# Small products in TensorE's first gaps, a later place for w_out's decode and the spatial tail's split, and another buffer for u's last weight chunk

## The chip, the cores and the metric

The kernel runs on one core of a Trainium2 chip. The metric is the device time in microseconds (us), taken as the median of several executions. Engines are named as in the profile: PE (TensorE matmul), PEld (its weight loads), DVE (VectorE), ACT (ScalarE), POOL (GpSimd) and SP (SyncE, which issues all the DMAs here).

## The reference

```python
def _attn_ref(q, k, v, g_norm):             # (8, 8, 576, 64)
    kv = np.einsum('bhsd,bhse->bhde', k, v)
    out = np.einsum('bhsd,bhde->bhse', q, kv)
    rms = np.sqrt(np.mean(out * out, axis=-1, keepdims=True) + 1e-06)
    return out / rms * g_norm

def _moe_ref(x, w_in, w_spatial, b_spatial, w_out):   # x: (8, 576, 512)
    h = np.maximum(x @ w_in, 0.0)
    u, v = h[..., :d_ff // 2], h[..., d_ff // 2:]
    v_n = (v - mean(v)) / np.sqrt(var(v) + 1e-06)
    v_s = np.einsum('ts,bsd->btd', w_spatial, v_n) + b_spatial[None, :, None]
    return (u * v_s) @ w_out
```

Linear attention without a softmax, eight batches of eight heads, normalized by head; then a gated network on the eight heads side by side: a product with `w_in` (512 x 1024), a layer norm of its second half v, a product with the 576 x 576 spatial weights along the sequence, the gate u times that, and a product with `w_out` (512 x 512). `w_in` and `w_out` are 64-bit floats and are handed over as raw words.

## The kernel before

**Stages.** One batch after the other. For a batch b and a pair of heads p: `att_k` multiplies k by v (`pskv`, L128) and copies the result to SBUF (L131, L132); `att_qa` multiplies q by it (`pso`, L188), squares it (ACT L171 by head with an accumulated sum, or L174 with a DVE sum L175) and begins the inverse root (L150 to L152); `att_qb` finishes it and scales (L157 to L159, x at L180); `att_t` transposes x on PE (`pstr`, L216) and copies it to SBUF (L218 for batch 0, L209 and L210 later). The last 64 rows of a pair of batches go together (`pst`, `pstt`). Then `hv` makes v and its layer norm, `u_unit` makes u, `sp_steps` the spatial product, `out_unit` the product with `w_out`.

**Batch 0** is computed another way, in plain fp32, while the weights still come in: `hv_32` (`psh`, L355) takes one 128-row chunk k of x and of `w_in` and adds it to four banks, one for each 128 tokens c; `u_32` (`psu`, L379) does the same for u; `sp_32` (`psa`, L388, L389) uses the spatial weights as they were loaded. From batch 1 on each product is three products of high and low halves (L272, L305, L411), and the halves are made by a copy on ACT and a subtraction on DVE: `split_in` (L566, L567) for `w_in`, `split_ws` for the spatial weights, `split_tail` (L605 to L614) for the spatial weights' last 64 rows and the bias, `make_out` for `w_out`.

**Weights.** `weight64` decodes a chunk of 64-bit words to fp32: one ACT instruction (L557) and five on DVE (L558 to L562), for each of eight chunks of `w_in` (four for v, then four for u) and four of `w_out`. A chunk is loaded into a staging buffer: `stage1` (four buffers) takes v's chunks and then the spatial weights, `stage0` (two) u's chunks, `stage2` (one) u's third chunk and then each of the four chunks of `w_out`. When batch 0 is done, `gates` closes `stage0` and `stage1` and puts the gate's halves (`GH`, `GL`) and `w_out`'s (`WOH`, `WOL`) in their place.

**What sets the order.** `PLAN`, a string of tokens, calls these steps for batch 0 in the order written: J, K are `att_k`; A, D `att_qa` (D with the squares summed on ACT); B `att_qb`; T `att_t`; H `hv_32` (H30 is tokens 3, chunk 0); u `u_32`; s `sp_32`; W the next weight load; C the next decode; X, E, z the splits; P `gates`; R the split of u's gate; L allows one more load of q, k or v; N8 is eight products of a zero tile before anything has come in. A scheduler then orders each engine's instructions by its own model: an instruction that depends on little can stand much earlier than its place in the program. An instruction given to `tc.keep_in_program_order` stays behind those so marked before it on its engine. On the chip each engine runs its list in order, and SP issues the DMAs in its own order.

Of the kernel before, what the change touches and what calls it, by code (L numbers as in the profile page):

```python
# [8 lines left out]
F32 = mybir.dt.float32  # L9
F32R = mybir.dt.float32r  # L10
U32 = mybir.dt.uint32
I32 = mybir.dt.int32
AF = mybir.ActivationFunctionType
ALU = mybir.AluOpType
# [3 lines left out]
DM, FF = 512, 1024  # L18
FH = FF // 2
P = 128  # L20
NP = H // 2
NC = S // P
TAIL = S - NC * P
# [8 lines left out]
HALF = DM // 2  # L32
NB = B
PLAN = """
N8 W L J00 D00 L W G J01 B00 C A01 L W L J02 T00 H00 C H10 H20 H30 B01 W C D02 J03 T01 Z H01 H11 H21 H31 C
L W B02 D03 T02 H02 H12 H22 H32 W B03 C d0 T03 H03 H13 H23 H33 b0 W L e0 e1 e2 e3 C L K10 C W t0 K11 C
u00 u01 u02 u03 F0 L K12 F1 W W L K13 F2 W W W d1 b1 F3 u10 X0 u11 X1 u12 L A10 X2 u13 t1 X3 L B10 A11 h E0
T10 s L B11 E1 T11 s A12 s L B12 z X4 s T12 A13 X5 s B13 L X6 s T13 W L X7 s s P R
"""


def f32(ap):
    return ap.bitcast(F32)
# [3 lines left out]
def body(ctx: ExitStack, tc, qT, kvm, kvt, g2, w_in, wsT, bsp, w_out, out):  # L47
    nc = tc.nc
    w_in = w_in.bitcast(U32)
    w_out = w_out.bitcast(U32)  # L50
# [9 lines left out]
    def persistent(shape, dt, name):  # L60
        return const.tile(shape, dt, name=name, tag=name)
# [10 lines left out]
    WTH = persistent([P, S], F32R, "WTH")  # L72
    WTL = [persistent([P, S], F32R, f"WTL{i}") for i in range(2)]
# [4 lines left out]
    R = [vpool.tile([P, 14 * HF], F32, name=f"R{x}", tag=f"V{x}") for x in "HL"]  # L78
# [7 lines left out]
    KVB = [persistent([P, P], F32, f"KVB{i}") for i in range(2)]  # L86
# [208 lines left out]
    def hv(b, c):  # L295
        ps = ps_mm.tile([P, 512], F32, name="psh", tag="mm")
        for k in range(NP):
            hv_k(c, k, ps)
        hv_end(c, ps)
# [7 lines left out]
    def split(hi, lo, x):  # L307
        nc.scalar.copy(hi, x)  # L308
        nc.vector.tensor_tensor(lo, x, f32(hi), op=ALU.subtract)  # L309
# [26 lines left out]
    def hv_tail():  # L336
        ps = ps_mm.tile([P, 512], F32, name="psh", tag="mm")
        cols = slice(NT, XC)
        three(ps, [m for k in range(NP) for m in
                   hl(XH[:, k, cols], XL[:, k, cols], WIH[:, k, FH:FF], WIL[:, k, FH:FF])])  # L340
        v = work.tile([P, FH], F32, name="v", tag="v", bufs=3)
        layer_norm(ps, v, nc.vector)
        d = work.tile([P, HS], F32, name="d", tag="g")[:, 0:HF]
        nc.vector.tensor_tensor(d, v[:, 0:HF], v[:, HF:FH], op=ALU.subtract)
        for x, cols in (v, slice(0, FH)), (d, slice(FH, FH + HF)):
            for i in range(2):
                own = slice(i * TAIL, (i + 1) * TAIL)
                other = slice((1 - i) * TAIL, (2 - i) * TAIL)
                hi = TA[i][own, cols]
                nc.scalar.copy(hi, x[own])  # L350
                nc.vector.tensor_copy(TB[i][own, cols], x[own])
                nc.vector.tensor_tensor(TA[i][other, cols], x[own], f32(hi), op=ALU.subtract)
# [31 lines left out]
    def sp_32(d, j):  # L384
        ps = ps_mm.tile([P, 512], F32, name="psa", tag="mm")[:, 0:HS]
        ds, cols = slice(d * P, (d + 1) * P), slice(j * HS, (j + 1) * HS)
        for c in range(NC):
            nc.tensor.matmul(ps, V32[:, c, ds], staged["s", c][:, cols], start=c == 0, stop=False)  # L388
        nc.tensor.matmul(ps, VT32[0:TAIL + 1, ds], WT32[0:TAIL + 1, cols], start=False, stop=True)  # L389
        nc.vector.tensor_tensor(U[:, d, cols], ps, U[:, d, cols], op=ALU.mult)  # L390
# [130 lines left out]
    GH = GL = WOH = WOL = None  # L521
    stage2 = ctx.enter_context(tc.tile_pool(name="stage2", bufs=1))
    staging = [ExitStack(), ExitStack()]
    stage0 = staging[0].enter_context(tc.tile_pool(name="stage0", bufs=2))
    stage1 = staging[1].enter_context(tc.tile_pool(name="stage1", bufs=4, side="right"))
    V32 = stage0.tile([P, NC, FH], F32, name="V32", tag="V32", bufs=1)
    WT32 = stage0.tile([P, S], F32, name="WT32", tag="WT32", bufs=1)
    staged, psu = {}, {}

    def load64(src, i, pool):  # L530
        staged[i] = pool.tile([P, 2 * DM], U32, name="stage", tag="stage")
        nc.sync.dma_start(staged[i], src)

    def load_in(half, k):
        i = NP * (1 - half) + k
        load64(w_in[k * P:(k + 1) * P, 2 * half * FH:2 * (half + 1) * FH], i,
               stage1 if half else stage2 if k == 2 else stage0)

    def load_ws(c):
        staged["s", c] = stage1.tile([P, 2 * DM], F32, name="stage", tag="stage")  # L540
        nc.sync.dma_start(staged["s", c][:, 0:S], wsT[c * P:(c + 1) * P, :])

    def load_tail():
# [2 lines left out]
            nc.sync.dma_start(WT32[r:r + 1], bsp)  # L546

    def load_out(k):
        load64(w_out[k * P:(k + 1) * P, :], 2 * NP + k, stage2)

    def weight64(i):

        wide = staged.pop(i).rearrange("p (f two) -> p f two", two=2)
        w0, w1 = wide[:, :, 0], wide[:, :, 1]
        to = W32[i] if i < 2 * NP else f32(w1)
        t = work.tile([P, DM], U32, name="t", tag="stg", bufs=2)
        nc.scalar.activation(f32(t), f32(w1), AF.Abs, scale=2.0 ** -112)  # L557
        nc.vector.tensor_scalar(t, t, 3, None, op0=ALU.logical_shift_left)  # L558
        nc.vector.scalar_tensor_tensor(w1, w1, 0x80000000, t, op0=ALU.bitwise_and, op1=ALU.bitwise_or)
        nc.vector.tensor_scalar(t, w1, 0xFF800000, None, op0=ALU.bitwise_and)  # L560
        nc.vector.scalar_tensor_tensor(f32(w0), w0, 2.0 ** -52, f32(t), op0=ALU.mult, op1=ALU.mult)
        nc.vector.tensor_tensor(to, f32(w1), f32(w0), op=ALU.add)  # L562
        return to

    def split_w(hi, lo, x):
        tc.keep_in_program_order(nc.scalar.copy(hi, x))  # L566
        tc.keep_in_program_order(nc.vector.tensor_tensor(lo, x, f32(hi), op=ALU.subtract))  # L567
# [3 lines left out]
        split_w(WIH[:, n % NP, fs], WIL[:, n % NP, fs], W32[n])  # L571

    def make_out(k):
        split_w(WOH[:, k, :], WOL[:, k, :], weight64(2 * NP + k))

    def split_ws(k):

# [24 lines left out]

    def split_tail():
        rows, other, r = slice(0, TAIL), slice(TAIL, P), TAIL + 32
        tc.keep_in_program_order(nc.scalar.copy(WTH[rows], WT32[rows]))  # L605
        nc.vector.tensor_tensor(WTL[0][rows], WT32[rows], f32(WTH[rows]), op=ALU.subtract)
        nc.scalar.copy(WTH[other], WT32[rows])
        nc.scalar.copy(WTL[1][other], f32(WTL[0][rows]))
        for n in (TAIL, r):
            nc.scalar.copy(WTL[0][n:n + 1], WT32[n:n + 1])  # L610
        low = WTL[0][r:r + 1]
        nc.vector.tensor_tensor(low, WT32[r:r + 1], f32(low), op=ALU.subtract)
        for n in (TAIL, r):
            nc.scalar.copy(WTL[1][n - TAIL:n - TAIL + 1], f32(WTL[0][n:n + 1]))  # L614

    todo = [(b + (kind != "f"), p, kind) for b in range(0, B, 2) for kind in "fkq"
            for p in range(NP)]
# [9 lines left out]
    def ahead(n=1):  # L627
        wanted[0] += n
        issue()
# [11 lines left out]
    def warm(n):  # L641

        ps = ps_tail.tile([P, 512], F32, name="psw", tag="tail")
        for _ in range(n):
            nc.tensor.matmul(ps[:, 0:P], KVB[1], KVB[1], start=True, stop=True)

    queue = []

    def enqueue(b, late=0):
# [3 lines left out]
    def step(n=1):  # L653
        for _ in range(n):
            if queue:
                queue.pop(0)()

    def gates():
        nonlocal GH, GL, WOH, WOL
        staging[0].close()  # L660
        pool = ctx.enter_context(tc.tile_pool(name="gates", bufs=1))
        GH, GL = (pool.tile([P, 4, XC], F32R, name=n, tag=n) for n in ("GH", "GL"))
        staging[1].close()
        outw = ctx.enter_context(tc.tile_pool(name="outw", bufs=1, side="right"))
        WOH, WOL = (outw.tile([P, NP, DM], F32R, name=n, tag=n) for n in ("WOH", "WOL"))

    loads = [lambda k=k: load_in(1, k) for k in range(NP)]
    loads += [lambda k=k: load_in(0, k) for k in range(NP)]
# [5 lines left out]
    psv = [ps_mm.tile([P, 512], F32, name="psh", tag="mm") for _ in range(NC)]  # L674
    st = [states.setdefault(b, {}) for b in range(2)]
    do = {
        "N": warm,
        "L": lambda: ahead(), "W": lambda: loads.pop(0)(), "C": lambda: weight64(makes.pop(0)),
        "K": lambda b, p: att_k(b, p, st[b]), "A": lambda b, p: att_qa(b, p, st[b]),
        "B": lambda b, p: att_qb(b, p, st[b]), "T": lambda b, p: att_t(b, p, st[b]),  # L680
# [5 lines left out]
        "F": lambda c: normalize(V32[:, c], nc.vector),  # L686
        "G": lambda: nc.sync.dma_start(gcol, g2), "h": hv_tail_32, "u": u_32,
        "s": lambda: sp_32(*units.pop(0)), "X": split_in, "E": split_ws, "z": split_tail,
        "Z": blank_tails, "P": gates, "R": split_g,
    }  # L690
    for token in PLAN.split():
        do[token[0]](*map(int, token[1:]))
# [3 lines left out]
    def first(b):  # L696

        for c in (0, 2, 1, 3):
            hv(b, c)
            step()  # L700
        for d in range(4):
            if d == 1 and b % 2 == 0:
                step(len(queue))
                hv_tail()
            elif d == 2 and b % 2:
                enqueue(b + 1)
                enqueue(b + 2)
            for j in range(2):
                u_unit(b, d, j)
                step()  # L710
            if b == 1:
                make_out(d)
                if loads:
                    loads.pop(0)()
    def second(b):
# [5 lines left out]
    def last(b):  # L721
        for c in [0, 1] + [NC] * (b % 2) + [2, 3]:
            out_unit(b, c)
            step()

    first(1)
    last(0)
    second(1)
# [53 lines left out]
```

## Time and profile before

| | us |
|---|---|
| median of 3 runs | 531.82 |
| the runs | 531.82, 529.98, 1777.45 |
| the profiled execution | 531.08 |
| its span, first to last instruction | 529.3 |
| mean granted clock of TensorE in it | 0.984 |

In a timeline row stand the start and the busy time (us), the engine, the source line, the operation, output <- input, the shape and the count; in brackets, how long the engine was idle before and what released it. A row of stages has the stretch and its length, the busy time (and instructions) of PE alone or of PE, PEld, DVE, ACT and POOL, the granted clock of TensorE, the busy share of the DMA engines and GB/s.

### The profile page before, as it was taken

Reading aid. Unit: us, or ns where it says so; the run is one execution under the profiler, and the core shown is the slowest. Engines: PE = TensorE matmul, PEld = TensorE weight load, DVE = VectorE, ACT = ScalarE, POOL = GpSimd, SP = SyncE. Lnnn points to the kernel's source line nnn. Section 1 sums busy time; section 2 is a strip of 40 time slices with the busy share of each in tenths; the row PEclk is TensorE's granted clock in tenths of the full one; section 3 lists DMA queues with packets and bytes.
Section 4 is the critical chain, followed back from the end, with each engine's and each line's share of the span. In section 5 each row is a group of like instructions: output and inputs, shape, how many; then the busy total and the mean of one; then the engine's idle time right before and its main releaser. Section 6 shows DMA issues by size and latency. Waiting matters only on the chain.

```text
span 529.3 us, 9377 instructions
## 1 busy us (share of the span) xinstructions
PE 514.7 (97%) x3496; PEld 449.6 (85%) x3496; DVE 359.9 (68%) x1089; ACT 241.5 (46%) x629; POOL 9.1 (2%) x25
## 2 busy tenths in 40 slices
PE   6978999999999999999999999999999999999997
PEld 5635867798998899989998899979998889988995
DVE  2799299879692697828693489918586289937480
ACT  3494365555542364335443356424444256334321
POOL 5000000000000000000000000000000000000000
PEclk8689999999999999999999999999999999999999
DMA  8963310242407102020424401120432300010003
GB/s 265 358 204 133 106 40 23 63 162 99 159 12 253 41 1 63 24 79 23 163 81 149 152 20 26 42 79 1 157 108 70 132 20 15 8 63 18 0 2 100
DMA packets 22305, 46.50 MB, mean 88 GB/s; under 512 B 2866, under 2 KB 7474, under 8 KB 22260
## 3 DMA queue, kind: packets, MB, share of 16 engines
q1 hardware_dynamic: 22260, 45.91, 26.4%
q8 instruction: 27, 0.44, 0.3%
q14 instruction: 18, 0.15, 0.1%
HBM read 36.46 MB, written 9.44 MB: 87 GB/s over the span
## 4 chain that ended last, share of the span: by engine, by line
PE 87%; DVE 7%; DMA 2%; ACT 2%; issue 1%; SPq 0%; ACTq 0%; DVEq 0%
PE pso L272 19%; PE psu L272 17%; PE psh L305 13%; PE psb L411 5%; PE pso L188 5%; PE psa L411 4%; PE pskv L128 4%; PE psc L411 4%; PE psu L379 2%; PE pstr L216 2%; PE psa L388 2%; PE psh L355 2%; PE psh L272 2%; DMA stage<-w_out 1%; PE pst L141 1%; DMA KV<-kvm 1%
## 5 line engine op out<-in xcount | busy, mean ns | idle before, releaser
L272 PE MATMUL psu<-XH,WIH 128*128 128x288 f32 x224 | 66.9, 299 | 0.0
L272 PE MATMUL psu<-XL,WIH 128*128 128x288 f32 x224 | 66.1, 295 | 0.0
L272 PE MATMUL psu<-XH,WIL 128*128 128x288 f32 x224 | 66.0, 295 | 0.0
L272 PE MATMUL pso<-WOH,GH 128*128 128x512 f32 x144 | 58.3, 406 | 0.2
L272 PE MATMUL pso<-WOL,GH 128*128 128x512 f32 x144 | 56.6, 394 | 0.0
L272 PE MATMUL pso<-WOH,GL 128*128 128x512 f32 x144 | 54.3, 396 | 0.0
L284 DVE BATCH_NORM_STATS2 s<-v 128x6 f32<-128x512 f32 x32 | 22.0, 692 | 41.8 <-ACT v L278 41.6
L438 ACT CAST GH<-g 128x288 fp32r<-128x288 f32 (+2 forms) x84 | 26.3, 351 | 42.7 <-DVE g L430 42.6
L305 PE MATMUL psh<-WIH,XH 128*128 128x512 f32 x112 | 44.4, 397 | 0.0
L305 PE MATMUL psh<-WIL,XH 128*128 128x512 f32 x112 | 43.8, 391 | 0.0
L305 PE MATMUL psh<-WIH,XL 128*128 128x512 f32 x112 | 42.8, 391 | 0.0
L272 PEld LDWEIGHTS psu<-XH,WIH 128*128 128x128 f32 x224 | 42.0, 188 | 0.7
L272 PEld LDWEIGHTS psu<-XL,WIH 128*128 128x128 f32 x224 | 42.0, 188 | 0.2
L272 PEld LDWEIGHTS psu<-XH,WIL 128*128 128x128 f32 x224 | 42.0, 188 | 0.0
L402 ACT ACTIVATE U<-psu 128x288 f32<-128x288 f32 x56 | 23.0, 411 | 33.4 <-PE psu L272 32.5
L512 ACT COPY o<-pso 128x512 f32<-128x512 f32 x35 | 19.7, 588 | 40.0 <-PE pso L272 37.7
L309 DVE TENSOR_TENSOR VL<-v,VH 128x512 fp32r<-128x512 f32 (+1 forms) x56 | 33.7, 617 | 6.2 <-ACT VH L308 5.7
L175 DVE TENSOR_REDUCE ss<-x 128x8 f32<-128x512 f32 x35 | 23.8, 681 | 19.1 <-ACT x L174 18.8
L308 ACT CAST VH<-v 128x512 fp32r<-128x512 f32 (+1 forms) x56 | 30.4, 564 | 11.1 <-DVE v L331 5.5
L272 PEld LDWEIGHTS pso<-WOH,GL 128*128 128x128 f32 x144 | 27.0, 188 | 5.7
L272 PEld LDWEIGHTS pso<-WOH,GH 128*128 128x128 f32 x144 | 27.0, 188 | 5.4 <-DVE g L430 0.6
L272 PEld LDWEIGHTS pso<-WOL,GH 128*128 128x128 f32 x144 | 27.1, 188 | 4.6
(185 smaller groups left out, 1228.5 us busy)
## 6 DMA issues: line engine op xcount, KB each, us to landing
KV<-kvm SPq DMA_DIRECT2D x31, 512.0 KB, 4.5
out<-o SPq DMA_DIRECT2D x32, 256.0 KB, 2.1
qt<-qT SPq DMA_DIRECT2D x16, 288.0 KB, 2.9
stage<-w_in SPq DMA_DIRECT2D x8, 512.0 KB, 6.9
qt<-qT SPq DMA_DIRECT2D x16, 256.0 KB, 2.6
KT<-kvt SPq DMA_DIRECT2D x32, 64.0 KB, 4.8
stage<-w_out SPq DMA_DIRECT2D x4, 512.0 KB, 3.4
stage<-wsT SPq DMA_DIRECT2D x4, 288.0 KB, 6.2
```

Of the source, the lines that this page charges most:

```text
L128: nc.tensor.matmul(ps[h, h], of[:, 0, h], of[:, 1, h], start=c == 0, stop=c == NC)
L175: nc.vector.tensor_reduce(ss, heads(x), axis=AX.X, op=ALU.add)
L188: nc.tensor.matmul(ps[:, c * P:(c + 1) * P], qt[:, c * P:(c + 1) * P], st[p], start=True, stop=True)
L272: nc.tensor.matmul(ps, lt, rh, start=i == 0, stop=i == n - 1)
L284: nc.vector.bn_stats(s6, v)
L305: nc.tensor.matmul(ps, lt, rh, start=k == 0 and i == 0, stop=k == NP - 1 and i == 2)
L308: nc.scalar.copy(hi, x)
L309: nc.vector.tensor_tensor(lo, x, f32(hi), op=ALU.subtract)
L402: nc.scalar.activation(U[:, d, cols], ps[:, 0:HS], AF.Relu)
L411: nc.tensor.matmul(ps, lt, rh, start=start and i == 0, stop=stop and i == len(pairs) - 1, skip_group_check=True)
L438: nc.scalar.copy(GH[:, d, dst], g[:, src])
L512: nc.scalar.copy(o, ps)
```

## The change

1. A new step `filler(n)`, token n: n products of 128 x 128 of the tile `KVB[1]` with itself, into the first 128 columns of the bank that `hv_32` uses for tokens 3 and has not begun. `PLAN` has n6 behind J00, n8 behind D00, n6 behind J01 and n6 behind A01. `KVB[1]` is zero until J01 has copied its product into it.
2. `PLAN` moves D02 and D03 to other places, moves weight loads (W), and puts the w_out chunks 0 and 1 in it: Q0 and Q1 (`make_out`, now the decode alone) before X0 and behind X5, O0 and O1 (`split_out`) behind P. The decodes of chunks 2 and 3 stay in `first(1)`.
3. The first two instructions of the decode of w_out's chunks 0 and 1, and all of `split_tail`, are marked to stay in program order; two of its copies change places.
4. Buffers: u's fourth chunk goes to `stage1` and not `stage0`; the fourth spatial chunk and w_out's chunk 1 go to `stage0`. `gates` is cut in two: `outw` (P) closes `stage1` and makes `WOH`, `WOL`; `gates` (p), behind the splits O0 and O1, closes `stage0` and makes `GH`, `GL`.

```diff
-N8 W L J00 D00 L W G J01 B00 C A01 L W L J02 T00 H00 C H10 H20 H30 B01 W C D02 J03 T01 Z H01 H11 H21 H31 C
+N8 W L J00 n6 D00 L n8 W G J01 n6 B00 C A01 L n6 W L J02 T00 H00 H10 D02 C H20 H30 B01 W C J03 T01 Z H01 H11 D03 H21 H31 W C
...
-               stage1 if half else stage2 if k == 2 else stage0)
+               stage2 if i == NP + 2 else stage1 if half or k == 3 else stage0)
...
+        pool = stage1 if c < 3 else stage0
...
-        load64(w_out[k * P:(k + 1) * P, :], 2 * NP + k, stage2)
+        load64(w_out[k * P:(k + 1) * P, :], 2 * NP + k, stage0 if k == 1 else stage2)
...
-        nc.scalar.activation(f32(t), f32(w1), AF.Abs, scale=2.0 ** -112)
-        nc.vector.tensor_scalar(t, t, 3, None, op0=ALU.logical_shift_left)
+        keep = tc.keep_in_program_order if i in (2 * NP, 2 * NP + 1) else lambda ins: ins
+        keep(nc.scalar.activation(f32(t), f32(w1), AF.Abs, scale=2.0 ** -112))
+        keep(nc.vector.tensor_scalar(t, t, 3, None, op0=ALU.logical_shift_left))
...
-        split_w(WOH[:, k, :], WOL[:, k, :], weight64(2 * NP + k))
+        decoded[k] = weight64(2 * NP + k)
+
+    def split_out(k):
+        split(WOH[:, k, :], WOL[:, k, :], decoded.pop(k))
...
+    def filler(n):
+        for _ in range(n):
+            tc.keep_in_program_order(
+                nc.tensor.matmul(psv[3][:, 0:P], KVB[1], KVB[1], start=True, stop=True))
...
+    def outw():
+        nonlocal WOH, WOL
         staging[1].close()
...
-            if b == 1:
-                make_out(d)
+            if b == 1 and d < 2:
+                make_out(2 + d)
+                split_out(2 + d)
```

PE at the program's start, from the first product of k and v (J00) to the second product of q (A01); `KVB_95` and `KVB_96` are `KVB[0]` and `KVB[1]`. Rows with a + are new:

```order
 L128 MATMUL pskv<-KT_103 64x64 x2
+L656 MATMUL psh<-KVB_96 128x128 x6
 L188 MATMUL pso<-KVB_95,qt 128x128 x4
 L141 MATMUL pst<-KVB_95,qt 128x128
+L656 MATMUL psh<-KVB_96 128x128 x8
 L128 MATMUL pskv<-KV_102 64x64 x8
 L128 MATMUL pskv<-KT_104 64x64 x2
+L656 MATMUL psh<-KVB_96 128x128 x6
 L188 MATMUL pso<-KVB_96,qt 128x128 x4
 L141 MATMUL pst<-KVB_96,qt 128x128
+L656 MATMUL psh<-KVB_96 128x128 x6
```

Four blocks, 26 products, now stand between the attention products; the third reads `KVB[1]` behind J01 and so takes J01's copied product, not zeros.

ACT before, from the decode of a u chunk to the copy of the last transposed chunk of batch 0 (RH is x of batch 0, WT the loaded spatial tail):

```order
L557 ACTIVATE t<-stage 128x512
L607 CAST WTH<-WT_121 64x576
L610 CAST WTL_81<-WT_121 1x576 x2
L218 ACTIVATE RH<-pstr,gcol 128x512
L171 ACTIVATE x,ss<-pst 128x64 x8
L614 CAST WTL_82<-WTL_81 1x576 x2
L566 CAST WIH<-RL 128x512
L150 ACTIVATE sh<-ss,epsc 128x8
L557 ACTIVATE t<-stage 128x512 x2
L218 ACTIVATE RH<-pstr,gcol 128x512
```

The same place of the changed kernel, from the decodes of u's last two chunks on:

```order
L559 ACTIVATE t<-stage 128x512 x2
L171 ACTIVATE x,ss<-pso 128x64 x8
L218 ACTIVATE RH<-pstr,gcol 128x512
L171 ACTIVATE x,ss<-pst 128x64 x6
L150 ACTIVATE sh<-ss,epsc 128x8
L171 ACTIVATE x,ss<-pst 128x64 x2
L150 ACTIVATE sh<-ss,epsc 128x8
L218 ACTIVATE RH<-pstr,gcol 128x512
```

The tail's casts (L607 to L614), one split of `w_in` (L566) and the second of the two decodes (L557 x2, the first chunk of w_out) are gone from between the two copies of RH; the squares of D03 now stand ahead of the first of them.

SP before, from the third load of k and v (for J02) to the fourth (for J03) and the load of `w_in` behind it:

```order
L108 DMA KV_101<-kvm 128x1024
L109 DMA KT_103<-kvt 64x256
L118 DMA qt<-qT 128x576
L532 DMA stage<-w_in 128x1024
L108 DMA KV_102<-kvm 128x1024
L109 DMA KT_104<-kvt 64x256
L532 DMA stage<-w_in 128x1024
```

and in the changed kernel:

```order
L108 DMA KV_101<-kvm 128x1024
L109 DMA KT_103<-kvt 64x256
L532 DMA stage<-w_in 128x1024 x2
L118 DMA qt<-qT 128x576
L532 DMA stage<-w_in 128x1024 x2
L113 DMA qs<-qT 128x128
L532 DMA stage<-w_in 128x1024
L108 DMA KV_102<-kvm 128x1024
L109 DMA KT_104<-kvt 64x256
L532 DMA stage<-w_in 128x1024
```

Five loads of `w_in`, of half a megabyte each, now stand between the two loads of k and v, where one stood. From the second batch's spatial product on, the engines' lists are the same in both kernels.

More of the change, by code (lines that the diff above doesn't have):

```diff
@@ L34 @@
 PLAN = """
-N8 W L J00 D00 L W G J01 B00 C A01 L W L J02 T00 H00 C H10 H20 H30 B01 W C D02 J03 T01 Z H01 H11 H21 H31 C
-L W B02 D03 T02 H02 H12 H22 H32 W B03 C d0 T03 H03 H13 H23 H33 b0 W L e0 e1 e2 e3 C L K10 C W t0 K11 C
-u00 u01 u02 u03 F0 L K12 F1 W W L K13 F2 W W W d1 b1 F3 u10 X0 u11 X1 u12 L A10 X2 u13 t1 X3 L B10 A11 h E0
-T10 s L B11 E1 T11 s A12 s L B12 z X4 s T12 A13 X5 s B13 L X6 s T13 W L X7 s s P R
+N8 W L J00 n6 D00 L n8 W G J01 n6 B00 C A01 L n6 W L J02 T00 H00 H10 D02 C H20 H30 B01 W C J03 T01 Z H01 H11 D03 H21 H31 W C
+W B02 L T02 H02 H12 H22 H32 W B03 C W d0 T03 H03 H13 H23 H33 b0 e0 e1 e2 e3 C L K10 C t0 L K11 C
+u00 u01 u02 u03 F0 L K12 F1 W W L K13 F2 W W W W d1 b1 F3 u10 Q0 u11 X0 u12 L A10 X1 u13 t1 X2 L B10 A11 h X3
+T10 s L B11 E0 T11 s A12 s L B12 E1 z s T12 A13 X4 W s B13 L X5 Q1 s T13 X6 L s X7 s P O0 O1 p R W
 """
@@ L527, in body @@
     WT32 = stage0.tile([P, S], F32, name="WT32", tag="WT32", bufs=1)
-    staged, psu = {}, {}
+    staged, decoded, psu = {}, {}, {}
     def load64(src, i, pool):
@@ L536, in load_in @@
         load64(w_in[k * P:(k + 1) * P, 2 * half * FH:2 * (half + 1) * FH], i,
-               stage1 if half else stage2 if k == 2 else stage0)
+               stage2 if i == NP + 2 else stage1 if half or k == 3 else stage0)
     def load_ws(c):
-        staged["s", c] = stage1.tile([P, 2 * DM], F32, name="stage", tag="stage")
+        pool = stage1 if c < 3 else stage0
+        staged["s", c] = pool.tile([P, 2 * DM], F32, name="stage", tag="stage")
         nc.sync.dma_start(staged["s", c][:, 0:S], wsT[c * P:(c + 1) * P, :])
@@ L604, in split_tail @@
         rows, other, r = slice(0, TAIL), slice(TAIL, P), TAIL + 32
[L605 to L608, printed above, removed]
+        keep = tc.keep_in_program_order
+        low = WTL[0][r:r + 1]
+        keep(nc.scalar.copy(WTH[rows], WT32[rows]))
+        keep(nc.vector.tensor_tensor(WTL[0][rows], WT32[rows], f32(WTH[rows]), op=ALU.subtract))
+        keep(nc.scalar.copy(WTH[other], WT32[rows]))
         for n in (TAIL, r):
-            nc.scalar.copy(WTL[0][n:n + 1], WT32[n:n + 1])
-        low = WTL[0][r:r + 1]
-        nc.vector.tensor_tensor(low, WT32[r:r + 1], f32(low), op=ALU.subtract)
+            keep(nc.scalar.copy(WTL[0][n:n + 1], WT32[n:n + 1]))
+        keep(nc.vector.tensor_tensor(low, WT32[r:r + 1], f32(low), op=ALU.subtract))
+        keep(nc.scalar.copy(WTL[1][other], f32(WTL[0][rows])))
         for n in (TAIL, r):
-            nc.scalar.copy(WTL[1][n - TAIL:n - TAIL + 1], f32(WTL[0][n:n + 1]))
+            keep(nc.scalar.copy(WTL[1][n - TAIL:n - TAIL + 1], f32(WTL[0][n:n + 1])))
     todo = [(b + (kind != "f"), p, kind) for b in range(0, B, 2) for kind in "fkq"
@@ L658, in gates @@
     def gates():
-        nonlocal GH, GL, WOH, WOL
+        nonlocal GH, GL
         staging[0].close()
@@ L662, in gates @@
         GH, GL = (pool.tile([P, 4, XC], F32R, name=n, tag=n) for n in ("GH", "GL"))
+    def outw():
+        nonlocal WOH, WOL
         staging[1].close()
-        outw = ctx.enter_context(tc.tile_pool(name="outw", bufs=1, side="right"))
-        WOH, WOL = (outw.tile([P, NP, DM], F32R, name=n, tag=n) for n in ("WOH", "WOL"))
+        pool = ctx.enter_context(tc.tile_pool(name="outw", bufs=1, side="right"))
+        WOH, WOL = (pool.tile([P, NP, DM], F32R, name=n, tag=n) for n in ("WOH", "WOL"))
     loads = [lambda k=k: load_in(1, k) for k in range(NP)]
@@ L676, in body @@
     do = {
-        "N": warm,
+        "N": warm, "n": filler,
         "L": lambda: ahead(), "W": lambda: loads.pop(0)(), "C": lambda: weight64(makes.pop(0)),
@@ L688, in body @@
         "s": lambda: sp_32(*units.pop(0)), "X": split_in, "E": split_ws, "z": split_tail,
-        "Z": blank_tails, "P": gates, "R": split_g,
+        "Z": blank_tails, "P": outw, "p": gates, "Q": make_out, "O": split_out, "R": split_g,
     }
```

## The prediction

> **What bounds the kernel.** First the page's head and busy times, then PE by stages: before u of batch 0 begins (48.48), the middle, the tail.
>
> ```profile
> span 529.3 us, 9377 instructions
> PE 514.7 (97%) x3496; PEld 449.6 (85%) x3496; DVE 359.9 (68%) x1089; ACT 241.5 (46%) x629; POOL 9.1 (2%) x25
> ...
> 26.80:42.00 15.20, 12.78 (x58) 6.66 (x58) 14.72 (x40) 12.00 (x48) 0.00 (x0) 0.89 0.62 203
> 48.48:500.00 451.52, 449.94 (x3122) 401.65 (x3121) 314.10 (x972) 207.42 (x504) 1.64 (x3) 1.00 0.23 73
> 500.00:529.30 29.30, 25.36 (x148) 22.52 (x146) 11.61 (x31) 6.77 (x18) 0.00 (x0) 1.00 0.14 46
> 105.00:125.00 20.00, 20.00 (x185) 18.80 (x183) 16.25 (x54) 11.78 (x28) 0.00 (x0) 1.00 0.38 127
> ```
>
> From 48.48 to 500 PE lacks 1.58 us of being busy all the time, at full clock. Since the lists differ only up to about 130 us and the products stay, the change can win only what PE loses before 48.48, and a part of that 1.58. Before 48.48 it loses in two ways. One is the clock; stages of PE alone (length, busy time, granted clock, DMA share, GB/s):
>
> ```profile
> 4.90:8.35 3.45, 1.06 (x20) 1.00 1.07 353
> 8.36:11.77 3.41, 2.92 (x19) 0.50 1.04 360
> 11.77:15.18 3.41, 2.88 (x25) 0.50 0.95 280
> 15.18:18.59 3.41, 3.04 (x28) 0.50 1.01 343
> 18.59:22.00 3.41, 3.41 (x4) 0.50 1.04 393
> 32.23:35.64 3.41, 1.34 (x6) 1.00 1.00 350
> 35.65:39.06 3.41, 3.41 (x5) 0.50 0.06 25
> 42.47:45.90 3.43, 2.45 (x6) 1.00 0.50 177
> ```
>
> The clock changes only at borders 3.41 us apart, and by the stretch just ended: busy 1.06 or 1.34 of it, half clock follows; 2.45, it stays full; 2.88 to 3.04 do not bring it back, 3.41 does. So it is at half from 8.36 to 22.00, and for one stretch from 35.65. The other loss is idle time; PE's own rows:
>
> ```profile
> 8.85 2.08 PE L188 MATMUL pso<-KVB,qt 128*128 128x128 f32 x8 [0.57 <-ACT KVB L132]
> ...
> 18.53 5.41 PE L355 MATMUL psh<-RL,RH 128*128 128x512 f32 x8 [0.36 <-ACT RH L218]
> 23.77 1.05 PE L188 MATMUL pso<-KVB,qt 128*128 128x128 f32 x8
> ...
> 24.98 0.69 PE L128 MATMUL pskv<-KV 128*64 128x64 f32 x16
> ...
> 25.71 0.65 PE L216 MATMUL pstr<-ident,x 128*128 128x128 f32 x4
> ...
> 28.44 3.70 PE L355 MATMUL psh<-RL,RH 128*128 128x512 f32 x8
> 33.20 0.63 PE L216 MATMUL pstr<-ident,x 128*128 128x128 f32 x4 [1.06 <-DVE qh L152]
> 34.93 5.40 PE L355 MATMUL psh<-RL,RH 128*128 128x512 f32 x8 [1.10 <-ACT RH L218]
> ...
> 43.45 3.70 PE L355 MATMUL psh<-RL,RH 128*128 128x512 f32 x8 [1.37 <-ACT RH L218]
> ...
> 48.48 6.09 PE L379 MATMUL psu<-RH,RL 128*128 128x288 f32 x24
> ```
>
> The last three waits, 3.5 us together, end in the copy RH on ACT or in the norm on DVE, and DVE is busy 14.72 of the 15.20 us from 26.80. What stands in their way there, on ACT, then on DVE (the last row, with three rows that give DVE's pace):
>
> ```profile
> 32.10 0.67 ACT L607 CAST WTH<-WT 64x576 fp32r<-64x576 f32 x1
> 32.80 1.36 ACT L610 CAST WTL<-WT 1x576 fp32r<-1x576 f32 x2
> ...
> 36.54 1.35 ACT L614 CAST WTL<-WTL 1x576 fp32r<-1x576 f32 x2
> ...
> 42.16 0.66 ACT L557 ACTIVATE t<-stage 128x512 f32<-128x512 f32 x1 [2.86 <-DMA stage<-w_out]
> ```
> ```profile
> 27.70 0.43 DVE L558 TENSOR_SCALAR t<-t 128x512 uint32<-128x512 uint32 x1
> 28.04 0.69 DVE L562 TENSOR_TENSOR RL<-stage 128x512 f32<-128x512 f32 x1
> 28.64 0.69 DVE L559 SCALAR_TENSOR_TENSOR stage<-stage,t 128x512 uint32<-128x512 uint32 x1
> ...
> 35.44 0.76 DVE L612 TENSOR_TENSOR WTL<-WT,WTL 1x576 fp32r<-1x576 f32 x1
> ```
>
> So 3.38 us of casts of the spatial tail, and a decode that sits 2.86 us at the head of ACT's queue until w_out's first chunk has landed, with RH behind it. In the changed lists all of these are behind batch 0's copies.
>
> **The change, part by part.** Fillers. A product of 128 x 128 is two records; the row at 8.85 gives 0.26 us a record at half clock, the start from 23.77 to 24.98 (ten records) 0.12 at full clock. The first n6 begins where J00 ends, 8.28 (8.85 less 0.57), at half clock: 12 x 0.26 = 3.1, so D00 begins at 11.4 and not 8.85: 2.55 late. In return PE is busy through the whole stretch 8.36 to 11.77, and the clock rises at 11.77 and not at 22.00. At full clock: D00 to 12.6, its tail product 12.8, n8 (16 x 0.12) 14.7, J01 (0.73, from 24.98 to 25.71) 15.4. The third block does not fill the hole behind J01: it reads KVB[1] and waits for the same copies as A01, 0.45, and then delays it by 1.45. A01 ends at 18.5, n6 at 20.0, J02 20.7, T00 21.1, D02 22.4, the four products of H for chunk 0 (3.70) 26.1. The same work ended at 24.98 before: by here the fillers have given back 1.1 us more than the clock won, and that is counted.
>
> Loads. Before, J03's k and v took this long to land:
>
> ```profile
> KV<-kvm SPq DMA_DIRECT2D x1, 512.0 KB, 6.3
> ```
>
> They were issued at about 12.4 and landed at 18.7. Now four more half-megabyte chunks are ahead: 2.1 MB at 343 to 393 GB/s (the stretches above, DMA share 1.0) is 5.3 to 6.1 us, so they land at 24.1 to 24.8, before J03 is wanted at 26.1. I take 0; the cover is 1.3 us. Behind it in SP's queue stand u's last chunk (buffer stage1, freed by the first decode), needed on ACT ahead of D03's squares: about 1.5 us later, still early.
>
> DVE. Its pace is 0.34 us for a decode's first and third step, 0.60 for a large one, 0.09 for a small one. Its changed list puts the u decodes ahead of norms. From 15.3, when the second decode's ACT step is done, to the x of A01 it has 13 large, 8 short and 7 small ones, 11.2 us: 26.7 with a wait of 0.3 for A01's squares. J03 ends at 26.8, T01 at 27.25; hence nothing lost.
>
> ACT's turn. The squares of a D step take 1.75 us, a copy RH 0.70:
>
> ```profile
> 10.96 1.75 ACT x L171 x16
> ...
> 17.79 0.70 ACT RH L218
> ```
>
> RH of chunk 1 at 27.95, H to 31.65, D03 to 32.6, T02 to 33.3. D03's squares now go ahead of chunk 2's RH: 32.6 + 1.75 + 0.70 = 35.05. PE waits 1.75 there: the wait that takes the place of the two of 1.06 and 1.10. H for chunk 2 ends at 38.75; T03's x, by ACT's six squares of the tail (1.3), the root and DVE, is there at about 38; RH 39.9, while K10 and the transposed tail fill PE to 40.4. The last H ends at 44.1, against 47.15 (43.45 + 3.70): **-3.0**.
>
> A second fall of the clock. The 1.75 lie in the stretch 32.24 to 35.65 if the borders are as here: PE busy about 1.65 of it, between 1.34 (fell) and 2.45 (stayed). A fall costs half a stretch, 1.7; I take half of that, **+0.85**, and keep 0 and 1.7 for the range. In the trace two waits of 1.06 and 1.10, in one stretch, were enough for the clock to fall.
>
> The Trainium skill, TensorE: Matmul & The Clock Gate, section "Why this matters for your kernels", asks only that gaps stay under about 3 us and has one idle window bring half clock. By it the fall at 35.65 would not have come, against this trace, nor would the new one, and the sum would be 0.85 lower; the trace decides. The same page (Part 1: The HAM clock gate) calls the window free-running and the point of the rise different from run to run; no run here shows a second phase.
>
> The phase. If the borders lie elsewhere the clock rises up to 3.4 later, when a whole stretch behind 8.28 is full: n8 then runs partly at half clock, A01 and with it DVE's list come up to 2 us later. The kernel before moves with the phase too. I take a quarter, **+0.5**.
>
> Later waits:
>
> ```profile
> 67.88 0.63 PE L226 MATMUL pstt<-ident,x 128*128 128x128 f32 x4 [0.53 <-DVE qh L152]
> ...
> 84.75 2.21 PE L388 MATMUL psa<-stage,V 128*128 128x288 f32 x8 [0.45 <-DVE U L390]
> ...
> 104.72 0.63 PE L216 MATMUL pstr<-ident,x 128*128 128x128 f32 x4 [0.43 <-DVE x L180]
> ```
> ```profile
> 94.84 2.39 ACT L308 CAST GH<-U 128x576 fp32r<-128x576 f32 x4
> ```
> ```profile
> stage<-w_out SPq DMA_DIRECT2D x4, 512.0 KB, 3.4
> ```
>
> The first chain is unchanged and stays. The second shortens, because three spatial splits leave DVE ahead of U, for one split of w_in. The third goes: A13 is now ahead of the last spatial unit's end, so its norm has some 8 us of products over it, and the w_out decode no longer stands in it. **-0.9**. The gate's split (the row at 94.84, with four subtractions on DVE of some 0.76 each by the 576-wide row L612) moves from 95 to about 109, behind the closing of stage0. In 105 to 125 DVE had 3.75 us free and ACT 8.2, and one decode of w_out (2.5 on DVE) leaves; the cover is that the first product with GH comes at about 122. I take 0; gone, it costs PE up to 1 through u's banks, where ACT copies u out behind that split.
>
> w_out and the tail. The tail's split and the two early decodes lie beside PE work between 50 and 100, where PE has its 1.58 us of waits in all; 0, with +0.5 as the other end. On SP, the loads of w_out's chunks 1 and 0 wait for u's decodes, at about 35 on DVE's list; behind them in that queue stands the load for K12, which PE wants only in the u stage, 10 us on. Chunk 2 needs stage2, so it is issued behind O0, at about 96, and takes 3.4 (last row): 99.5. Its decode is ahead of the copy of T13's transposed x on ACT, which comes at about 102; the cover is 3 us, and if it is gone PE waits as at 104.72, 0.4 or more.
>
> **Sum:** -3.0 + 0.85 + 0.5 - 0.9 = -2.55. The profiled execution took 531.08, its span 529.28 and 1.8 around it: 531.08 - 2.55 = 528.5. The median of the runs is 531.82, 0.7 above; I keep to the profiled one.
>
> **Rivals.** (1) Nothing is won: the second fall comes (+0.85 more), the clock rises a stretch late (+1.5 more), or J03's load lands 1 to 2 late: 530 to 532. For it: 1.65 is nearer 1.34 than 2.45, and DVE's list has no slack from 15 on. (2) Slower: the filler does not fill its stretch (waits between its products, or a product of zeros does not count) and the clock stays at half. Then D00 ends at 13.5, n8 (4.2) with the tail product at 18.2, J01 at 19.7, n6 (3.1) at 23.2, A01 at 25.3 and not 18.3, and DVE's list comes 7 later, the last H at 51.1: 531.08 + 3.95 - 0.9 = 534.1. It decides between 3.04 and 3.41 busy in the stretch. Against it: eight such products of zeros ran ahead of 4.9, and the clock was full then. (3) More is won: no second fall, an early border, and the wait of 0.53 goes too: -3.0 - 0.9 - 0.53 - 0.5 = -4.9, 526. (4) The change doesn't do what it says: the third block fills no hole; that is in the sum.
>
> **Numbers.** Forecast 0.60, nothing won 0.20, more won 0.12, slower 0.08. The range 525.5 to 532.5 takes in the ends of the first three. Faster by over 2% (about what a measurement of this kernel can tell from no change, 10.6 us) would need most of what PE loses before 48.48: 14.6 idle in all less 1.58 and the tail's 3.94 is 9.1, a part of it before any data has come, and half of 17.1 at half clock is 8.5. I give it 0.02. Slower by 2%: 0.02. Within: 0.96.
>
> **What would show it.** Clock full from about 12 to 15 on; H for chunk 0 ended at 25 to 27; T02's RH behind D03's squares with PE waiting 1 to 2 us; the last H ended at 43 to 46; u begun at about 45.5; no wait on w_out before 100; PE still full from there. It is wrong if the clock is at half past 16, if J03 waits for its load, or if a wait of over 1 us appears between 85 and 130.

## The result and the profile after

| | before | after |
|---|---|---|
| median of 6 runs, one chip | 531.35 us | 527.76 us (526.86 to 529.62) |
| ratio, 95% interval | | 0.9943 [0.9917, 0.9969] |
| forecast | | 528.5 us (525.5 to 532.5), same |
| profiled execution, its span | 531.08, 529.3 | 529.62, 527.8 |

The change won about 3 us, 0.6%, by the ratio, and 3.6 by the medians; the run of before that took 1777.45 us is not in the ratio. The profiled execution of after was the longest of its six runs. First its page's head and busy times:

```profile
span 527.8 us, 9482 instructions
PE 516.2 (98%) x3548; PEld 453.8 (86%) x3548; DVE 360.5 (68%) x1089; ACT 241.3 (46%) x629; POOL 9.1 (2%) x25
```

PE has 52 records more, the 26 filler products. PE's timeline of the same execution, with the fillers (L656) and the waits:

```profile
8.48 2.93 PE L656 MATMUL psh<-KVB 128*128 128x128 f32 x12
11.20 1.72 PE L188 MATMUL pso<-KVB,qt 128*128 128x128 f32 x8
...
12.98 1.95 PE L656 MATMUL psh<-KVB 128*128 128x128 f32 x16
...
16.19 1.60 PE L656 MATMUL psh<-KVB 128*128 128x128 f32 x12 [0.52 <-ACT KVB L132]
...
22.73 3.60 PE L355 MATMUL psh<-RL,RH 128*128 128x512 f32 x8
26.25 0.69 PE L128 MATMUL pskv<-KV 128*64 128x64 f32 x16
...
27.85 0.66 PE L216 MATMUL pstr<-ident,x 128*128 128x128 f32 x4 [0.80 <-DVE x L180]
29.29 5.40 PE L355 MATMUL psh<-RL,RH 128*128 128x512 f32 x8 [0.78 <-ACT RH L218]
...
37.99 3.70 PE L355 MATMUL psh<-RL,RH 128*128 128x512 f32 x8 [1.75 <-ACT RH L218]
...
43.28 3.60 PE L355 MATMUL psh<-RL,RH 128*128 128x512 f32 x8
...
67.60 0.63 PE L226 MATMUL pstt<-ident,x 128*128 128x128 f32 x4 [0.53 <-DVE qh L152]
```

The first block runs at half clock (2.93 us for 12 records, 0.24 each), the second at full clock (0.12 each); D00's products in between take 1.72 and not 1.06, so the clock rises about 12.6. The third block waits 0.52 and fills no hole. Chunk 0 of H ends at 26.25 (an end of H is here the start of PE's next instruction, 0.1 to 0.2 before start plus busy time), chunk 1 takes 5.40 and not 3.70, and the last H ends at 46.81. Behind 48 us one wait is left of three. PE by stretches (length, busy, granted clock, DMA share, GB/s):

```profile
26.26:29.67 3.41, 1.83 (x26) 1.00 0.84 260
29.67:33.08 3.41, 3.41 (x5) 0.50 0.91 301
...
36.50:39.91 3.41, 1.92 (x5) 1.00 0.48 135
48.48:500.00 451.52, 450.83 (x3131) 1.00 0.23 72
```

A second fall of the clock is here, and it costs the 1.70 us that H of chunk 1 takes longer. From 48.48 on PE loses 0.69 us, and lost 1.58 before.

On ACT, from the second RH of batch 0's chunks to the fourth, neither the tail's casts nor w_out's decode stand any more; D03's squares are ahead of the third (rows of after, the third and fourth RH):

```profile
37.20 0.74 ACT L218 ACTIVATE RH<-pstr,gcol 128x512 f32<-128x512 f32 x1
...
42.16 0.69 ACT L218 ACTIVATE RH<-pstr,gcol 128x512 f32<-128x512 f32 x1 [2.07 <-PE pstr L216]
```

### The profile page after: what moved, and what is told of

Same layout as the page of the kernel before. It is cut to its first block, busy times and chain, and to the rows that moved or that the text cites. A ratio compares the mean times of both kernels' runs of the same rounds, so it can differ in the third digit from the quotient of the medians.

```text
span 527.8 us, 9482 instructions
## 1 busy us (share of the span) xinstructions
PE 516.2 (98%) x3548; PEld 453.8 (86%) x3548; DVE 360.5 (68%) x1089; ACT 241.3 (46%) x629; POOL 9.1 (2%) x25
## 4 chain that ended last, share of the span: by engine, by line
PE 93%; DVE 3%; ACT 1%; DMA 1%; issue 0%; SPq 0%; DVEq 0%
PE pso L272 19%; PE psu L272 17%; PE psh L305 15%; PE psb L411 6%; PE pso L188 5%; PE pskv L128 4%; PE psa L411 4%; PE psc L411 4%; PE psh L355 3%; PE psa L388 3%; PE pstr L216 2%; PE psu L379 2%; PE psh L272 2%; PE psh L656 1%; PE pst L141 1%; DMA KV<-kvm 1%
```

## The experiments

Ratios are to the kernel before, run on the same chip in the same call; chips differ (medians of before: 529.81, 530.94 and 529.77 us in the three calls). All kernels compute the whole reference; the fillers' results are overwritten.

### The two halves of the change: no fillers, fillers alone

Theory A: the gain comes from clearing ACT and DVE between 30 and 43 us, and the fillers give back what their clock wins. Rival B: the gain is the early clock.

```diff
 u1_no_fill, against the changed kernel
-N8 W L J00 n6 D00 L n8 W G J01 n6 B00 C A01 L n6 W L J02 ...
+N8 W L J00 D00 L W G J01 B00 C A01 L W L J02 ...
 e2_fill_only, against the kernel before
-N8 W L J00 D00 L W G J01 B00 C A01 L W L J02 ...
+N8 W L J00 n6 D00 L n8 W G J01 n6 B00 C A01 L n6 W L J02 ...
```

> The changed kernel without the four blocks of small products. Theory A (most of the gain comes from taking the spatial tail's split and w_out's first decode out of ACT's and DVE's way between 30 and 43 us, and the small products give back what the clock wins): 527 to 529, the same as the changed kernel (527.76) within 1 us. Rival B (the gain is the clock that rises ten microseconds sooner): 530.5 or more, close to before (531.35). In the profile the clock should be at half until about 18 to 22 us under both.

> The kernel before with the four blocks of small products at the same four places and nothing else. Theory A: 530.5 to 532.5, no gain. Rival B: 527.5 to 529.

Without the fillers: 524.80 us, 0.9917 [0.9895, 0.9939]. With the fillers alone: 530.56 us, 1.0011 [0.9994, 1.0029]. PE of the kernel without fillers:

```profile
18.59 3.70 PE L355 MATMUL psh<-RL,RH 128*128 128x512 f32 x8 [0.51 <-ACT RH L218]
...
37.62 3.70 PE L355 MATMUL psh<-RL,RH 128*128 128x512 f32 x8
```

Its clock is at half until about 17.5, five us longer than after's, and still chunk 0 begins 4.1 us earlier and the last H ends at 41.15. The time is below the 527 to 529 of theory A: by the ratios the fillers cost some 1.3 us, though the intervals overlap. PE of the kernel with fillers alone (its profiled execution, 528.98 us, was the fastest of its twelve):

```profile
34.80 3.70 PE L355 MATMUL psh<-RL,RH 128*128 128x512 f32 x8 [1.81 <-ACT RH L218]
```

Its clock rises early too, at about 12, and by the ratio no time is won: RH still waits, and both later waits stay (0.44 at 82.16 and 0.55 at 102.23). B falls: the fillers don't win, the rest of the change does.

### Why the fillers cost: lists, not only products

```diff
 u3_two_fill, against the changed kernel
-N8 W L J00 n6 D00 L n8 W G J01 n6 B00 C A01 L n6 W L J02 ...
+N8 W L J00 n6 D00 L n8 W G J01 B00 C A01 L W L J02 ...
 w7_long_warm and y12_long_again, against u1_no_fill; x9_before_long, against the kernel before;
 x11_after_long, against the changed kernel (all four blocks)
-        "N": warm,
+        "N": lambda n: warm(n + 4),
```

> The changed kernel without the third and fourth block (behind J01 and A01), which fill no hole. If each block costs what it delays A01: 1.5 us (third block) is won, ratio 0.991 to 0.993. If the first two are the costly ones, or the order that the scheduler makes with them: 0.994 to 0.996, as the changed kernel.

> The changed kernel without the four blocks, but with twelve products ahead of the first data and not eight, so that PE is busy until the first k and v have landed; nothing else of the lists moves much. Theory A1 (the small products hurt because they stand between attention products on the path; a full clock from the start is worth 1 to 2 us by itself): 1 to 2 us below the version without the blocks (ratio 0.9917), so a ratio of 0.988 to 0.990, with the clock full from about 5 to 8 us on. Rival A2 (until about 25 us the loads set the pace and the clock is worth nothing): ratio 0.990 to 0.993.

> The kernel without filler blocks and with twelve zero products ahead of the first data, once more, on the chip of its neighbours in this call. If its gain is real and not a matter of one chip: 0.982 to 0.987, no later than 523.5 us, with a spread of under 1 us over the runs. If that was a chance of phase: 0.989 to 0.994 as without the four extra products.

> The changed kernel with all four filler blocks, and twelve zero products ahead of the first data and not eight. With the clock full from about 12, the blocks are 20 products (two blocks of six, one of eight, one of six less) of two records at 0.12 us and the first at 0.26: about 7 to 8 us of TensorE time in all, 2 of them in holes. If the blocks delay the path also at a full clock: 3 to 5 us behind the same kernel without blocks (0.9846), so 0.990 to 0.994, and not better than the change itself (0.9941) by more than 0.004. If the vector engine's list covers them: within 1 us of it, 0.983 to 0.987.

(The fillers are 26 products, 52 records, some 6.2 us at 0.12; the last text miscounts them.)

| | median, us | ratio, 95% interval |
|---|---|---|
| two blocks | 526.64 | 0.9930 [0.9909, 0.9951] |
| no block, twelve warm-up products | 522.34 | 0.9846 [0.9823, 0.9869] |
| the same, another chip | 524.89 | 0.9889 [0.9859, 0.9919] |
| four blocks, twelve warm-up products | 527.26 | 0.9956 [0.9938, 0.9974] |

Two blocks (0.9930) lie at the edge of the first forecast, and the interval reaches into the second: undecided. In their profile PE waits 0.99 for J03's load, which lands at 24.7.

The last two kernels of the table ran on one chip, and their intervals don't overlap: the blocks cost 0.0067, 3.5 us, when the warm-up is longer (2.4 by the medians). The profile of the last shows how. PE:

```profile
8.61 1.60 PE L656 MATMUL psh<-KVB 128*128 128x128 f32 x12
...
21.01 3.60 PE L355 MATMUL psh<-RL,RH 128*128 128x512 f32 x8
26.25 0.69 PE L128 MATMUL pskv<-KV 128*64 128x64 f32 x16 [1.64 <-DMA KV<-kvm]
...
40.60 3.60 PE L355 MATMUL psh<-RL,RH 128*128 128x512 f32 x8
```

The clock is full from the first block on (0.13 a record); chunk 0 of H ends at 24.61 (start plus busy time) and not at 26.25, and the last H ends at 44.13, no earlier than in the second profile of the change (44.15, below): PE waits 1.64 for J03's load. That load is late because of the blocks. With them the scheduled list issues more of the weights' chunks ahead of it: in the changed kernel, run again, five between J02's load and J03's (SP's queue):

```profile
8.41 0.33 SPq L108 DMA_DIRECT2D KV<-kvm  x1
...
9.36 1.35 SPq L532 DMA_DIRECT2D stage<-w_in  x2
...
12.58 0.91 SPq L532 DMA_DIRECT2D stage<-w_in  x2
...
14.49 0.33 SPq L532 DMA_DIRECT2D stage<-w_in  x1
14.92 0.38 SPq L108 DMA_DIRECT2D KV<-kvm  x1
```

and without blocks one:

```profile
8.24 0.33 SPq L108 DMA_DIRECT2D KV<-kvm  x1
...
11.97 0.43 SPq L532 DMA_DIRECT2D stage<-w_in  x1
12.65 0.33 SPq L108 DMA_DIRECT2D KV<-kvm  x1
```

With four blocks and the longer warm-up it is six; J03's load is issued at 16.21 and takes 9.9 us to land. J03's products begin at 26.25 there and at 21.65 in the first of the two profiles without blocks below: 4.60 later, of which the wait for the load is 1.64; the other 2.96 are the blocks' own time on PE, less what the earlier clock saves. With the chunks come their decodes on DVE, ahead of batch 0's norms; in the changed kernel, where PE is later, J03 doesn't wait for its load, but T01 waits 0.80 for A01's x behind these decodes (the row at 27.85 in after). So the blocks delay the products and, by the lists, the data that the products wait for; with either wait the last H ends at about 44.

The kernel with no block and twelve warm-up products is faster than the kernel before on both chips, and by the ratios than the changed kernel. Against the same without the four products (0.9917) the first chip's interval lies apart, the second's overlaps. Its two profiles differ in where the clock rises. PE of the first (span 520.7), then of the second (span 524.4):

```profile
13.42 1.16 PE L188 MATMUL pso<-KVB,qt 128*128 128x128 f32 x8 [0.52 <-ACT KVB L132]
...
35.61 3.70 PE L355 MATMUL psh<-RL,RH 128*128 128x512 f32 x8
```
```profile
13.35 2.08 PE L188 MATMUL pso<-KVB,qt 128*128 128x128 f32 x8 [0.53 <-ACT KVB L132]
...
18.94 5.34 PE L355 MATMUL psh<-RL,RH 128*128 128x512 f32 x8 [0.78 <-ACT RH L218]
...
39.32 3.70 PE L355 MATMUL psh<-RL,RH 128*128 128x512 f32 x8
```

A01's eight records take 1.16 us in the one and 2.08 in the other, where the clock rises only at about 22.3, 9.5 us later; the last H is 3.7 us later, and so is the end. The program is the same, so in this order 9.5 us of full clock are worth 3.7. PE by stretches, the first, then the second profile:

```profile
9.34:12.76 3.42, 3.42 (x30) 0.51 1.04 372
```
```profile
8.62:12.03 3.41, 2.98 (x20) 0.50 1.04 348
```

In the first the stretch begins behind the wait ahead of D00 and ends ahead of that before A01; PE is busy all through it, and the clock rises. In the second the borders lie 0.7 us earlier, a part of the wait ahead of D00 falls into the stretch, and the waits behind it into the next two (2.88 and 2.72 busy), until 18.86 to 22.27 (3.33 busy) brings the clock back. The longer warm-up therefore doesn't make the early rise certain: the second chip's runs spread from 521.66 to 526.15, the first's from 522.21 to 522.44.

### The early clock alone

> The kernel before with one edit: twelve zero products ahead of the first data and not eight, so that TensorE has no hole between them and J00 and the clock should be full by about 12 us. Theory C (the early clock by itself is worth what it showed when the same edit was made without the filler blocks, 0.9846 against 0.9917, some 3.8 us, on any order of the lists): 0.992 to 0.995 of the kernel before, the last H of batch 0 ended at about 43. Theory L (in the old order the vector and scalar engines' work of 28 to 43 us sets the end of batch 0's H, and a faster TensorE waits longer for it): 0.997 to 1.001, the last H ended at 45 or later, the waits on RH and on the norm longer by what the clock wins.

525.56 us, 0.9909 [0.9879, 0.9939]: by the ratio theory C, and past its range. The profile can't bear its reason out, for it is that of the slowest of the six executions (528.59; the others took 523.55 to 527.23). PE by stretches, then its last H, then ACT:

```profile
19.00:22.40 3.40, 3.22 (x4) 0.50 1.02 396
22.40:25.80 3.40, 3.40 (x23) 1.00 1.04 354
```
```profile
39.12 3.70 PE L355 MATMUL psh<-RL,RH 128*128 128x512 f32 x8
```
```profile
33.39 0.69 ACT L218 ACTIVATE RH<-pstr,gcol 128x512 f32<-128x512 f32 x1 [0.79 <-PE pstr L216]
35.74 1.36 ACT L610 CAST WTL<-WT 1x576 fp32r<-1x576 f32 x2
...
38.38 0.69 ACT L218 ACTIVATE RH<-pstr,gcol 128x512 f32<-128x512 f32 x1 [0.26 <-PE pstr L216]
...
41.73 0.67 ACT L557 ACTIVATE t<-stage 128x512 f32<-128x512 f32 x1
```

In this execution the clock rose at 22.40, where it rose before (22.00), and the last H still ended at 42.82 by start plus busy time, where it was 47.15. Four more products at the start also changed the scheduler's lists: RH of chunk 2 now stands ahead of two of the tail's casts, and RH of chunk 3 ahead of the decode of w_out (the row at 41.73). The waits of 1.06, 1.10 and 1.37 and the fall of the clock at 35.65 are gone, for one wait of 1.18 ahead of D03 and one of 0.78 ahead of H for chunk 2. That is theory A's mechanism once more, reached by accident. But it doesn't explain the median's gain of 4.2 us: this execution is only 1.2 below the median of before beside it (529.77), and from 49 to 130 us it loses 2.01, where before lost 1.41. The rest of the gain stands in the faster executions. Their mean granted clock is 0.990 to 1.000, the higher the faster, against 0.987 here, as an earlier rise would give it; none of them was profiled, so how much is the clock and how much the lists stays open.

### The pins

```diff
 u4_tail_free, against the changed kernel; w8_no_fill_free has it too, and u5's edit, without fillers
-        keep = tc.keep_in_program_order
-        keep(nc.scalar.copy(WTH[rows], WT32[rows]))
+        tc.keep_in_program_order(nc.scalar.copy(WTH[rows], WT32[rows]))
...
 u5_wout_free, against the changed kernel
-        keep = tc.keep_in_program_order if i in (2 * NP, 2 * NP + 1) else lambda ins: ins
+        keep = lambda ins: ins
```

> The changed kernel with the spatial tail's split free to stand early again (its six casts, 3.4 us of ACT, stand between RH of chunk 1 and the squares of D03). Theory A, with the tail as a large part of it: 529 to 530.5, and PE's wait for RH of chunk 2 or 3 grows by 1 to 3 us. Rival C (ACT waits for D03 there anyway, so the casts fill idle time): 527.5 to 528.5.

> The changed kernel with w_out's two early decodes left to the scheduler again (the tail's split stays pinned). In the scheduled lists the decode's step on the scalar engine comes behind batch 0's last RH of the four chunks anyway, since its load is issued later. If the place of the load and not the pin keeps it out of the way: as the change, 0.993 to 0.996, the last H at 44 to 45. If the pin is what won (2.86 us at the head of the scalar queue before): 0.997 to 1.000, with a wait on w_out or behind it of 1 us or more before 100 us.

> The changed kernel without the four blocks and with both the tail's split and w_out's first decode free to stand early again; what is left of the change are the places of D and W, the buffers and the splits of w_out behind batch 0. If pinning is what wins: ratio 0.995 to 1.0, 2 us or more above the version without the blocks (0.9917). If the rest wins: 0.991 to 0.993.

With the tail free, only its first cast is pinned, as in the kernel before, and the two copies are back in their places: 527.67 us, 0.9968 [0.9951, 0.9985]. The casts stand between the copies of RH again, and PE's wait ahead of H for chunk 2 is 2.24 and not 1.75. w_out's decode free: 527.21 us, 0.9949 [0.9934, 0.9964], as the change. Both free and no fillers: 526.93 us, 0.9933 [0.9908, 0.9957], with a wait for RH of 1.16 ahead of the last H. The pin on w_out's decode wins nothing that shows: without it the scheduler puts the decodes of chunks 0 and 1 right behind batch 0's last RH (42.72 and 43.79 on ACT). The load's time is not the reason, for the first of w_out's chunks is issued at 32.63 there and was at 38.68 before; why the scheduler now puts the decodes later isn't shown. (The profiled execution of this kernel, the longest of its eleven, has the second fall of the clock too.) The tail's pin may be worth about 1 us; the intervals with and without it overlap, both with fillers and without. Most of the gain is in the order of PLAN and in the buffers, which no run here tells apart.

The later waits tell the parts apart as well. PE from 49 to 130 us, in the kernel before, with the fillers alone, and in the changed kernel:

```profile
49.00:130.00 81.00, 79.59 (x492) 1.00 0.27 87
```
```profile
49.00:130.00 81.00, 79.35 (x493) 1.00 0.25 81
```
```profile
49.00:130.00 81.00, 80.47 (x499) 1.00 0.27 82
```

PE loses 1.41, 1.65 and 0.53 us. With either pin left out, and without fillers, it loses 0.53 too, and 1.17 with both pins left out and no fillers: these 0.9 us come mostly from PLAN and the buffers.

### The new wait behind D03's squares, and the change again

```diff
 v6_d03_late, against the changed kernel
-... J03 T01 Z H01 H11 D03 H21 H31 W C
-W B02 L T02 H02 H12 ...
+... J03 T01 Z H01 H11 H21 H31 W C
+W B02 L T02 D03 H02 H12 ...
 r_after: the changed kernel, unchanged
```

> The changed kernel with D03 behind T02, so that RH of chunk 2 stands ahead of D03's squares on ACT. If the 1.75 us that PE waits there in the changed kernel's profile are on the path: 526 to 527, and no wait ahead of H for chunk 2. If D03's norm, which then comes later, is the next to be late: 527.5 to 528.5 with a wait of 1 us or more ahead of T03 or H for chunk 3.

> The changed kernel as it is, run beside the others of this call. Its ratio to the kernel before was 0.9943 in the first measurement; the same is expected, 0.993 to 0.997.

With D03 behind T02: 526.79 us, 0.9948 [0.9929, 0.9967], no gain on the change. PE:

```profile
33.71 3.70 PE L355 MATMUL psh<-RL,RH 128*128 128x512 f32 x8
...
38.92 0.63 PE L216 MATMUL pstr<-ident,x 128*128 128x128 f32 x4 [1.51 <-DVE qh L158]
```

The 1.75 us ahead of chunk 2 are gone and 1.51 stand ahead of chunk 3; the last H ends at 44.23. The wait moved. The change again: 527.25 us, 0.9941 [0.9921, 0.9960]. PE in its profile (span 525.1):

```profile
28.32 3.70 PE L355 MATMUL psh<-RL,RH 128*128 128x512 f32 x8 [0.78 <-ACT RH L218]
...
44.15 0.68 PE L128 MATMUL pskv<-KV 128*64 128x64 f32 x14
```

The waits are those of the first profile of after (the 1.75 at 35.33 among them), but there is no second fall: chunk 1 takes 3.70, and the last H ends at 44.15.

## Why the prediction was right

- **Batch 0's H, -3.0: right.** The forecast was 44.1 for the last H without a fall, and the second profile of the change has 44.15. The first has 46.81: 1.70 from the fall and about 1 from the phase.
- **The second fall and the phase, +0.85 and +0.5: right as means.** In one profiled execution the fall cost 1.70 and the phase about 1, in the other neither cost anything, so half of the one and 0.5 for the other were fair choices; how often each comes isn't known. The place was wrong: the fall came in the stretch that ended at 29.67, with two waits of 0.80 and 0.78, and not in the one with the wait of 1.75.
- **The decodes ahead of the norms on DVE, nothing lost: not so.** PE waits 0.80 ahead of T01 for A01's x in both profiles of the change. In the second one x is ready at 26.83, as forecast (26.7), but PE had ended chunk 0 at 25.28, 0.8 earlier than forecast (26.1), and lost that again. The two cancel: that the last H came to 44.15 is in this part luck.
- **The new wait of 1.75 behind D03's squares: right, to 0.01.** With D03 later (v6) a wait of 1.51 stands one chunk later instead.
- **Later waits, -0.9: right.** The waits at 84.75 and 104.72 are gone (0.88), that at 67.88 stays. PE had no wait on w_out, nor one for the gate's split.
- **The fillers give back more than their clock wins: right, and too small.** The forecast was 1.1 us by the end of chunk 0. Removing them wins 1.3 us by the ratios, though those intervals overlap; with the longer warm-up it wins 3.5, and those don't. The prediction listed the four chunks ahead of J03's load but priced them at nothing, with 1.3 us of cover. The landing was well forecast for five chunks in all (24.1 to 24.8; 24.7 in u3), but with PE early J03 waits for that load, 0.99 in u3 and 1.64 in x11, where six chunks are ahead; so the cover was there only because the fillers had delayed PE.
- **The rule for the rise: right, and now narrower.** In every profile here whose half clock is on record, stretches with 3.04 us busy or less didn't bring the full clock back, and those with 3.22 or more did (3.22 in x9).
- **Casts of the tail and w_out's decode out of ACT's way: right in substance.** u1 bears it out, and by accident the lists of x9. That the pins do it isn't: w_out's decode stays out of the way without its pin.
- **The base.** The sum stood on an execution of before of 531.08. The median beside after was 531.35, so the forecast of -2.55 stands against -3.6 of the medians and -3.0 by the ratio.

Of the rivals, the first (nothing won) came only in part, in the profiled execution with the second fall and the later rise (529.62), and the second (the clock stays at half) didn't happen; the third (more won, 526) asked for no second fall and for the wait of 0.53 to go as well: the execution without the fall took 526.95, and the 0.53 stayed. The fourth, that the third block fills no hole, was so.

## What to carry to other kernels

Where a scheduler orders the lists, an instruction added for one engine moves loads and work of the others: read the new lists of every engine and price what moved before the price of the instruction itself. Idle-time filler was worth most here ahead of the first data, where nothing waits behind it, and least between products that the path needs. A ratio that fits a theory is not its proof, and neither is one profile: x9 had the ratio of the clock theory, and its only profile, with the clock unchanged, is that of its slowest execution. Look at where the profiled execution stands among the runs before reading a median's cause from it.

## What the runs showed of the hardware

**Where the clock rises differs between executions of one kernel.** The clock of the kernel without blocks and with twelve warm-up products (w7, y12) rose 9.5 us apart in its two profiles, worth 3.7 us of 521; what differed is where the borders of the stretches fell between nearly the same waits. The Trainium skill, TensorE: Matmul & The Clock Gate, Part 1 (The HAM clock gate), says that the window is free-running and the rise varies from run to run; the traces agree. Its sentence that the penalty is under 1% of a typical span agrees too (3.7 of 520.7 is 0.7%), but here that is more than the change won.

**The granted clock in the page can miss a half clock at the start.** In the profile of w8 (no fillers, both pins free), D00's row and the stretch that it lies in:

```profile
9.34 2.07 PE L188 MATMUL pso<-KVB,qt 128*128 128x128 f32 x8 [0.57 <-ACT KVB L132]
```
```profile
9.00:13.00 4.00, 3.66 (x30) 1.00 0.98 338
```

Its eight records take 0.26 us each, as at half clock, under a granted 1.00. Durations of like records are the safer reading. A mean of 1.00 can therefore hide a half clock at the start: the means fall in step with the times in x9, but don't sort the six executions of after (529.62 has 0.997, 527.07 has 0.995).

**Short waits were enough for a fall, a longer one was not.** In after's first profile the stretch with waits of 0.80 and 0.78 (busy 1.83 of 3.41) was followed by half clock, that with the single wait of 1.75 (busy 1.92) was not. 0.66 of the first stretch's busy time are transposes, and none of the second's is. The same page's section "Why this matters for your kernels" would have only gaps over about 3 us matter; the trace disagrees. Its Part 4 (PE-mode transpose) says that transposes don't count as busy in the same way, and by it the two stretches would be 1.17 against 1.92; that fits these two. It doesn't fit a stretch of the kernel with the fillers alone:

```profile
32.44:35.85 3.41, 1.60 (x8) 1.00 0.70 243
35.85:39.26 3.41, 3.41 (x23) 1.00 0.54 154
```

Of its 1.60 busy 0.56 are transposes, which leaves 1.04, less than 1.17, and the clock stayed full. Busy time, with or without the transposes, doesn't sort the falls; what does stays open.
